# Smaller first loads, tile by tile first products and another order of the head in a mixer and MLP kernel

## The chip, the core and the metric

The kernel runs on one core of a Trainium2 chip. The metric is the device time of one execution in microseconds (us), as a median of several runs. One more execution is taken by the hardware profiler; it gives the profile, and its own time and span are given beside the median. The core has a matmul engine (PE, with its weight loads shown apart as PEld), a vector engine (DVE), an activation engine (ACT), GpSimd (POOL), and SP, which here does nothing but issue DMA transfers.

## The reference

All inputs are bf16: x is 1 x 2048 x 512, w1 and w2 are 512 x 512, w3 is 512 x 1792 and w4 1792 x 512.

```python
h  = gelu(layernorm(x) @ w1)
c  = D // 4                      # four groups of 128 channels
g0 = h[:, :, 0:c]     shifted by +1 row      # zeros come in
g1 = h[:, :, c:2*c]   shifted by -1 row
g2 = h[:, :, 2*c:3*c] shifted by +2 rows
g3 = h[:, :, 3*c:]    shifted by -2 rows
x1 = x + concat(g0, g1, g2, g3) @ w2
out = x1 + gelu(layernorm(x1) @ w3) @ w4
```

The layernorm has no weights; its epsilon is 1e-5, and GELU is the tanh form.

## The kernel before, in words

**Tiling.** The 2048 rows are 16 tiles of 128, taken with a stride: partition p holds rows 16p to 16p+15, tile t is row 16p+t of each partition. A shift by rows is thus mostly a shift to a neighbouring tile. Two tiles make a pair, and the first product (w1) is done by pairs.

**Stages for a tile q of the first layernorm.** A load of x from SP (`load_x`, L253); statistics on DVE (`st`, L325) and their aggregate (`ag`, L328); the reciprocal root on POOL (`rs`, for two tiles at a time or one: an add, L349, and a power, L358); the normalisation on DVE (`norm`, L378) into `xn`. Then a transpose, in one of two ways. Tiles 0 to 7: four transposes on PE into a bank of PSUM (`tp`, L400) and an evacuation on ACT into `xT` (`evA`, L412). Tiles 8 to 15: a DMA transpose that SP issues (`dT`, L388). The first product of a pair (`m1`, L451) is four groups of four matmuls with a moving operand of 256 columns, one group for each 128 output channels. GELU on ACT (`g1`) writes `hT`, which holds the shifts. The second product of a tile (`m2 tile bank channels`, L526) reads `hT` of the pairs that its shifts reach, and `add` on DVE (L538) makes x1.

**After the head** follow x1's statistics, normalisation (mostly on ACT, L373) and DMA transposes, then the wide part: mm3 (L553), GELU (L566), mm4 (L579), the last add (L593) and the store (L597). mm3 starts with w3 and the first four transposed tiles of x1.

**What sets the order.** Each engine runs its instructions in the order in which the program calls the helpers. The helper records each operation with what it reads and writes (`Prog`), and `emit` turns these into semaphore waits. For the head, the order is written out by hand in the string `HEAD` (L160): each step is a name and its numbers, and each engine takes its own steps from it in order. A step stands on one engine only; an engine whose next step waits runs nothing else meanwhile. `dT` steps set SP's order, behind the loads, which stand ahead of the head (L617 to L627).

**Pair 0 before.** Its product is `m1i` (`mm1_by_input`, L459): one step per input chunk of w1, each with four matmuls of 256 columns, into the four banks 0 to 3, so that it can start with the first chunks of w1. It reads both tiles of the pair. `warm` (L604) is 12 and then 3 matmuls of constants ahead of the first transposes.

**Loads before.** x tiles 0, 1, 2 and 3 alone (128 KB each), 4 and 5 together (256 KB), w1 chunks 0 and 1 and then 2 and 3 (256 KB each), x tiles 6 and 7 (256 KB), 8 to 11 and 12 to 15 (512 KB each), w2 (512 KB): eleven transfers.

Of the kernel before, what the change touches and what calls it, by code (L numbers as in the profile page):

```python
# [5 lines left out]
P = 128  # L6
# [151 lines left out]


HEAD = """  # L160
st 0; ag 0; rs 0 1; st 1; ag 1; rs 1 1; st 2; st 3; ag 2; ag 3; warm 3 3 1; rs 2; norm 1; norm 0;
tp 1 5; tp 0 4; st 4; evA 1; norm 2; norm 3; evA 0; tp 2 6; tp 3 7; st 5; ag 4; ag 5; m1i 0 0 0;
evA 3; rs 4; m1i 0 0 1; evA 2; m1i 0 0 2; st 6; m1i 0 0 3; norm 4; m1 1 4 3; norm 5; g1 0;
tp 4 6; st 7; m1 1 4 0; ag 6; ag 7; tp 5 7; rs 6; evA 4; m1 1 4 1; st 9; evA 5; m1 1 4 2; st 8;
norm 7; m1 2 0 1; ag 8; ag 9; g1 1; m1 2 0 3; rs 8; norm 6; tp 7 7; st 11; m1 2 0 2; evA 7;
tp 6 6; norm 8; m1 2 0 0; ag 11; evA 6; m2 2 4 0; m2 2 4 1; st 10; m1 3 2 2; norm 9; ag 10; g1 2;
m1 3 2 0; rs 10; st 13; m1 3 2 1; m1 3 2 3; st 12; m2 2 4 2; dT 8; m2 2 4 3; norm 11; ag 13;
norm 10; g1 3; m2 3 5 0 1 2 3; st 14; ag 12; dT 9; rs 12; st 15; m2 4 6 0 1 2 3; ag 14; ag 15;
m1 4 0 3; rs 14; dT 11; m1 4 0 1; norm 13; m1 4 0 0; add 3; norm 14; dT 10; m2 5 7 0 1 2 3;
add 2; m1 4 0 2; norm 12; norm 15; dT 13; g1 4; dT 12; dT 14; dT 15  # L170
"""


def bass_standalone__mixer_s_mlp__prompt_kernel(
# [13 lines left out]
    DC = D // P  # L188
# [12 lines left out]
    with ExitStack() as es:  # L201
# [3 lines left out]
        xT = sb("xT", [P, DC, S], BF16)  # L205
# [3 lines left out]
        w1_sb = sb("w1_sb", [P, DC, D], BF16)  # L209
# [33 lines left out]
        g_mv = [Gen() for _ in range(2 * NT)]  # L243
# [5 lines left out]
        def bankap(b, n=1):  # L249
            return ps[:, 512 * b : 512 * (b + n)]  # L250


        def load_x(eng, t0, n):  # L253
            pr.op(eng, f"x{t0}",
                  lambda e: e.dma_start(x_sb[:, t0 : t0 + n, :], x3[:, t0 : t0 + n, :]),
                  w=g_x[t0 : t0 + n], dma=True)

        def load_w(name, dst, src, c0=0, n=DC):

            v = src.rearrange("(c p) f -> p c f", p=P)  # L260
            pr.op("sp", f"{name}_{c0}",
                  lambda e: e.dma_start(dst[:, c0 : c0 + n, :], v[:, c0 : c0 + n, :]),
                  w=[g_w[(name, c)] for c in range(c0, c0 + n)], dma=True)
# [103 lines left out]
        def norm(eng, q):  # L367
            a, g = src(q)
            s = q % NXN
            g_xn[q] = xn_slot[s].new()  # L370
            if eng == "act":
                pr.op("act", f"norm{q}",
                      lambda e: e.activation(xn[:, s, :], a, ACT_F.Identity,  # L373
                                             bias=nmr[:, q : q + 1], scale=rstd[:, q : q + 1]),
                      r=[g, g_nmr[q], g_rstd[q]], w=[g_xn[q]])
            else:
                pr.op(eng, f"norm{q}",
                      lambda e: e.tensor_scalar(xn[:, s, :], a, mv[:, q, 0:1], rstd[:, q : q + 1],  # L378
                                                ALU.subtract, ALU.mult),
                      r=[g, g_mv[q], g_rstd[q]], w=[g_xn[q]])  # L380

        def xT_of(q):
            return (xT, q) if q < NT else (x1T, q - NT)
# [22 lines left out]
        def evacT(eng, q):  # L406
            g, b = g_tp[q]
            dst, c = xT_of(q)
            a = ps_bf[:, 1024 * b : 1024 * b + 512].rearrange("p (c s) -> p c s", c=DC)
            o = dst[:, :, P * c : P * (c + 1)]  # L410
            if eng == "act":
                pr.op("act", f"ev{q}", lambda e: e.activation(o, a, ACT_F.Copy), r=[g], w=[g_xT[q]])  # L412
            else:
                pr.op("dve", f"ev{q}", lambda e: e.tensor_copy(o, a), r=[g], w=[g_xT[q]])
# [24 lines left out]
        g_y = {}  # L439
# [16 lines left out]
            pr.op("pe", f"mm1_{p}_{len(fcs)}", f, r=all_of("w1") + [g_xT[2 * p], g_xT[2 * p + 1]],  # L456
                  w=[gens[h] for h in range(2) if any(fc // 2 == h for fc in fcs)])

        def mm1_by_input(p, b, dcs):  # L459

            if p not in g_y:
                g_y[p] = ([bank[b + i].new() for i in range(DC)], b)
            for dc in dcs:
                def f(e, dc=dc):
                    for fc in range(DC):
                        dst = ps[:, 512 * (b + fc) : 512 * (b + fc) + 256]
                        ins = e.matmul(dst, w1_sb[:, dc, P * fc : P * (fc + 1)],
                                       xT[:, dc, 256 * p : 256 * (p + 1)],
                                       start=(dc == 0), stop=(dc == DC - 1))
                    return ins  # L470

                pr.op("pe", f"mm1_{p}_1_{dc}", f,
                      r=[g_w[("w1", dc)], g_xT[2 * p], g_xT[2 * p + 1]], w=g_y[p][0])

        def hap(j, p, jn=1):

# [127 lines left out]
        def keep_warm(n, b, after=()):  # L604

            g = bank[b].new()
            ones = nc.const_aps.tensor(1.0, (P, 512), BF16)

            def f(e):
                for _ in range(n):  # L610
                    ins = e.matmul(bankap(b), ones[:, 0:P], ones, start=True, stop=True)  # L611
                return ins

            pr.op("pe", f"warm{len(after)}", f, r=list(after), w=[g])
# [3 lines left out]
        load_x("sp", 1, 1)  # L618
        load_x("sp", 2, 1)
        load_x("sp", 3, 1)  # L620
        load_x("sp", 4, 2)
        load_w("w1", w1_sb, w1, 0, 2)
        load_w("w1", w1_sb, w1, 2, 2)
        load_x("sp", 6, 2)
        load_x("sp", 8, 4)
        load_x("sp", 12, 4)
        load_w("w2", w2_sb, w2)  # L627
# [58 lines left out]
        def last_tile():  # L686
# [6 lines left out]

        steps = {
            "st": stats, "ag": aggr, "rs": rstd_pool, "norm": lambda q: norm("dve", q), "tp": peT,
            "evA": lambda q: evacT("act", q), "dT": dmaT,
            "m1i": lambda p, b, *dcs: mm1_by_input(p, b, dcs),
            "warm": lambda n, b, q: keep_warm(n, b, [g_mv[q]]),
            "m1": lambda p, b, *fcs: mm1(p, b, fcs), "g1": gelu1,
            "m2": lambda t, b, *js: mm2(t, b, js), "add": add1,  # L700
        }
# [22 lines left out]
        for k in (10, 12, 14):  # L724
            q = NT + k
# [49 lines left out]
```

## Time and profile before

| what | us |
|---|---|
| median of 3 runs (138.76 to 138.92) | 138.88 |
| the profiled execution, its own time | 139.09 |
| its span in the profile | 137.3 |
| PE busy | 131.9 |
| DVE busy | 51.6 |
| ACT busy | 50.0 |
| first transpose on PE / first product on PE / first mm3 on PE | 6.76 / 8.73 / 38.03 |
| PE idle before the first two groups of transposes | 0.48 and 0.70 |
| landing of x tiles 8 to 11, issued at 4.56 | 11.6 |

The span goes from the first instruction to the last. All times in the profile count from its start. A row of a timeline has a start, a length from the first start to the last end, the engine, line and operation with what it writes and reads, the number of instructions, and in brackets the idle time of the engine before it with what ended it. Instructions of one engine overlap in their last part, so the step from one start to the next is shorter than an instruction's own length. "SPq" is the queue on which SP issues transfers; a landing is the time from issue to the last semaphore update. The granted PE clock was 1.0 over the whole profiled execution.

### The profile page before, as it was taken

Reading aid. Unit: us, or ns where it says so; the run is one execution under the profiler, and the core shown is the slowest. Engines: PE = TensorE matmul, PEld = TensorE weight load, DVE = VectorE, ACT = ScalarE, POOL = GpSimd, SP = SyncE. Lnnn points to the kernel's source line nnn. Section 1 sums busy time; section 2 is a strip of 40 time slices with the busy share of each in tenths; the row PEclk is TensorE's granted clock in tenths of the full one; section 3 lists DMA queues with packets and bytes.
Section 4 is the critical chain, followed back from the end, with each engine's and each line's share of the span. In section 5 each row is a group of like instructions: output and inputs, shape, how many; then the busy total and the mean of one; then the engine's idle time right before and its main releaser. Section 6 shows DMA issues by size and latency. Waiting matters only on the chain.

```text
span 137.3 us, 1790 instructions
## 1 busy us (share of the span) xinstructions
PE 131.9 (96%) x689; PEld 66.5 (48%) x701; DVE 51.6 (38%) x125; ACT 50.0 (36%) x60; POOL 18.3 (13%) x52
## 2 busy tenths in 40 slices
PE   7879999999999999999999999999999999999993
PEld 3267847664444444444444444444444444444452
DVE  0989899999976620000232000023200002232222
ACT  4068622399545555552000555300055530000000
POOL 2542442464312200000000000000000000000000
PEclk9999999999999999999999999999999999999999
DMA  4996144589955599300111100011110001111121
GB/s 106 289 283 238 27 93 82 111 261 351 133 100 113 83 287 257 103 5 0 38 38 38 38 0 5 0 38 38 38 38 0 5 0 38 38 38 38 38 74 41
DMA packets 20119, 12.16 MB, mean 89 GB/s; under 512 B 13712, under 2 KB 19088, under 8 KB 20112
## 3 DMA queue, kind: packets, MB, share of 16 engines
q1 hardware_dynamic: 19968, 12.03, 33.6%
q8 instruction: 5, 0.08, 0.3%
q10 hardware_dynamic: 144, 0.03, 0.1%
q14 instruction: 2, 0.02, 0.0%
HBM read 6.82 MB, written 2.10 MB: 65 GB/s over the span
## 4 chain that ended last, share of the span: by engine, by line
PE 83%; DVE 8%; DMA 4%; POOL 1%; issue 1%; DVEq 0%
PE ps L579 35%; PE ps L553 35%; PE ps L526 8%; PE ps L451 5%; DVE st L325 5%; DVE xn L378 2%; DMA x_sb<-in_x_dram 2%; DMA xT<-xn 2%; POOL rstd L358 1%; DVE mv L328 1%; POOL vpe L349 0%; DVE o_sb L593 0%; DVEq L134 0%
## 5 line engine op out<-in xcount | busy, mean ns | idle before, releaser
L579 PE MATMUL ps<-w_sb,h2T 128*128 128x512 bf16 (+2 forms) x234 | 48.7, 366 | 0.2
L553 PE MATMUL ps<-x1T,w_sb 128*128 128x512 bf16 x219 | 48.6, 379 | 0.3
L566 ACT ACTIVATE h2T<-ps 128x1024 bf16<-128x1024 f32 x28 | 28.6, 1023 | 44.8 <-PE ps L553 44.8
L593 DVE TENSOR_TENSOR o_sb<-ps,x_sb 128x512 bf16<-128x512 f32 (+2 forms) x17 | 11.2, 660 | 75.0 <-PE ps L579 75.0
L579 PEld LDWEIGHTS ps<-w_sb,h2T 128*128 128x128 bf16 x238 | 22.8, 98 | 25.9
L553 PEld LDWEIGHTS ps<-x1T,w_sb 128*128 128x128 bf16 x224 | 21.9, 98 | 26.4
L325 DVE BATCH_NORM_STATS2 st<-x_sb 128x6 f32<-128x512 bf16 x32 | 20.7, 675 | 2.3 <-DMA x_sb<-in_x_dram 2.3
L526 PE MATMUL ps<-w_sb,hT 128*128 128x512 bf16 x61 | 14.3, 379 | 0.2
L451 PE MATMUL ps<-xT,w_sb 128*128 128x256 bf16 x112 | 14.0, 273 | 0.3 <-DMA xT<-xn 0.3
L451 PEld LDWEIGHTS ps<-xT,w_sb 128*128 128x128 bf16 x112 | 10.6, 98 | 3.1 <-issue 0.7
L358 POOL TENSOR_TENSOR rstd<-vpe,neghalf 128x2 f32<-128x2 f32 (+1 forms) x17 | 11.8, 695 | 1.0
L538 DVE TENSOR_TENSOR x_sb<-ps,x_sb 128x512 bf16<-128x512 f32 x16 | 10.3, 678 | 0.3 <-PE ps L526 0.2
L378 DVE TENSOR_SCALAR xn<-x_sb,mv,rstd 128x512 bf16<-128x512 bf16 x22 | 8.3, 405 | 5.2 <-POOL rstd L358 5.0
L526 PEld LDWEIGHTS ps<-w_sb,hT 128*128 128x128 bf16 x64 | 6.2, 98 | 6.3 <-ACT hT L512 0.3
L373 ACT ACTIVATE xn<-x_sb,nmr,rstd 128x512 bf16<-128x512 bf16 x10 | 7.6, 807 | 3.3 <-POOL nmr L363 3.3
L512 ACT ACTIVATE hT<-ps 128x1024 bf16<-128x1024 f32 x6 | 6.1, 1019 | 6.1 <-PE ps L451 6.0
L349 POOL TENSOR_SCALAR vpe<-mv 128x2 f32<-128x2 f32 (+1 forms) x17 | 3.9, 229 | 27.3 <-DVE mv L328 27.2
L412 ACT ACTIVATE xT<-ps 128x512 bf16<-128x512 bf16 x8 | 4.5, 603 | 5.9 <-PE ps L400 5.9
L611 PE MATMUL ps<-const-bfloat16-1.0 128*128 128x512 bf16 x15 | 5.4, 522 | 0.9 <-PEq L760 0.8
L328 DVE BATCH_NORM_AGGREGATE mv<-st 128x2 f32<-128x6 f32 x32 | 4.9, 172 | 0.1
L400 PE MATMUL ps<-ident,xn 128*128 128x128 bf16 x32 | 3.0, 221 | 1.2 <-DVE xn L378 1.2
L611 PEld LDWEIGHTS ps<-const-bfloat16-1.0 128*128 128x128 bf16 x15 | 1.8, 127 | 4.0 <-issue 3.2
(18 smaller groups left out, 12.8 us busy)
## 6 DMA issues: line engine op xcount, KB each, us to landing
w_sb<-in_w_dram SPq DMA_DIRECT2D x4, 512.0 KB, 4.8
out_dram<-o_sb SPq DMA_DIRECT2D x15, 128.0 KB, 1.8
w_sb<-in_w_dram SPq DMA_DIRECT2D x1, 1792.0 KB, 7.3
x_sb<-in_x_dram SPq DMA_DIRECT2D x2, 512.0 KB, 7.5
w_sb<-in_w_dram SPq DMA_DIRECT2D x3, 256.0 KB, 4.1
x_sb<-in_x_dram SPq DMA_DIRECT2D x4, 128.0 KB, 2.5
x_sb<-in_x_dram SPq DMA_DIRECT2D x2, 256.0 KB, 4.1
x1T<-xn SPq DMA_TRANSPOSE x16, 3.6
```

Of the source, the lines that this page charges most:

```text
L325: pr.op("dve", f"st{q}", lambda e: e.bn_stats(st6[:, q, :], a), r=[g], w=[g_st[q]])
L358: lambda e: e.tensor_tensor(rstd[:, q : q + n], vpe[:, q : q + n], neghalf[:, 0:n], ALU.pow),
L373: lambda e: e.activation(xn[:, s, :], a, ACT_F.Identity, bias=nmr[:, q : q + 1], scale=rstd[:, q : q + 1]),
L378: lambda e: e.tensor_scalar(xn[:, s, :], a, mv[:, q, 0:1], rstd[:, q : q + 1], ALU.subtract, ALU.mult),
L451: ins = e.matmul(dst, w1_sb[:, dc, P * fc : P * (fc + 1)], xT[:, dc, 256 * p : 256 * (p + 1)], start=(dc == 0), stop=(dc == DC - 1))
L526: ins = e.matmul(bankap(b), hT[:, j, c : c + P], w2_sb[:, j, :], start=(j == 0), stop=(j == DC - 1))
L538: lambda e: e.tensor_tensor(x1_sb[:, t, :], bankap(b), x_sb[:, t, :], ALU.add),
L553: ins = e.matmul(bankap(b + i), w3_sb[:, dc, P * fc : P * (fc + 1)], x1T[:, dc, 512 * s : 512 * (s + 1)], start=(dc == 0), stop=(dc == DC ...
L566: pr.op("act", f"g2_{s}_{fp}", lambda e: e.activation(o, a, ACT_F.Gelu_apprx_tanh), r=gens, w=[g])
L579: ins = e.matmul(ps[:, 512 * b : 512 * b + n], h2T[:, fc, s % 2, P * i : P * (i + 1)], w4_sb[:, fc, c0 : c0 + n], start=(fc == 0), stop=(f ...
L593: lambda e: e.tensor_tensor(o_sb[:, s, 0:n], ps[:, 512 * b : 512 * b + n], x1_sb[:, t, c0 : c0 + n], ALU.add),
L611: ins = e.matmul(bankap(b), ones[:, 0:P], ones, start=True, stop=True)
```

## The change

It has three parts. The loads of x tiles 0 to 7 and of w1's four input chunks become twelve transfers of 128 KB, in the order x0, x1, x2, x3, x4, w1 chunk 0, chunk 1, x5, chunk 2, chunk 3, x6, x7; the three transfers of 512 KB behind them stay. `mm1_by_input` gives way to `mm1_tile_by_input`: the first products of tiles 0 and 1 are made for each tile by itself, four steps of four matmuls with 128 columns, into halves of the same banks 0 to 3. And `HEAD` is written anew: tile 0's normalisation, transpose and evacuation come ahead of tile 1's, tile 0's product stands ahead of transposes 3 and 2, and tile 1's product is mixed with them; tile 4's transpose is evacuated by DVE (`evD`) in place of ACT; the order of statistics, normalisations, groups of `m1` and `m2` and of the DMA transposes (9 ahead of 8) differs down to the end of the head, where `add 3` and `add 2` now stand behind all of the normalisations. What follows the head is as it was.

```diff
 HEAD = """
-st 0; ag 0; rs 0 1; st 1; ag 1; rs 1 1; st 2; st 3; ag 2; ag 3; warm 3 3 1; rs 2; norm 1; norm 0;
-tp 1 5; tp 0 4; st 4; evA 1; norm 2; norm 3; evA 0; tp 2 6; tp 3 7; st 5; ag 4; ag 5; m1i 0 0 0;
-evA 3; rs 4; m1i 0 0 1; evA 2; m1i 0 0 2; st 6; m1i 0 0 3; norm 4; m1 1 4 3; norm 5; g1 0;
-tp 4 6; st 7; m1 1 4 0; ag 6; ag 7; tp 5 7; rs 6; evA 4; m1 1 4 1; st 9; evA 5; m1 1 4 2; st 8;
-norm 7; m1 2 0 1; ag 8; ag 9; g1 1; m1 2 0 3; rs 8; norm 6; tp 7 7; st 11; m1 2 0 2; evA 7;
-tp 6 6; norm 8; m1 2 0 0; ag 11; evA 6; m2 2 4 0; m2 2 4 1; st 10; m1 3 2 2; norm 9; ag 10; g1 2;
-m1 3 2 0; rs 10; st 13; m1 3 2 1; m1 3 2 3; st 12; m2 2 4 2; dT 8; m2 2 4 3; norm 11; ag 13;
-norm 10; g1 3; m2 3 5 0 1 2 3; st 14; ag 12; dT 9; rs 12; st 15; m2 4 6 0 1 2 3; ag 14; ag 15;
-m1 4 0 3; rs 14; dT 11; m1 4 0 1; norm 13; m1 4 0 0; add 3; norm 14; dT 10; m2 5 7 0 1 2 3;
-add 2; m1 4 0 2; norm 12; norm 15; dT 13; g1 4; dT 12; dT 14; dT 15
+st 0; st 1; ag 0; rs 0 1; st 2; ag 1; st 3; rs 1 1; norm 0; ag 2; ag 3; warm 3 3 1; tp 0 4; rs 2;
+st 4; norm 1; evA 0; tp 1 5; st 5; m1x 0 0 0; ag 4; ag 5; m1x 0 0 1; evA 1; rs 4; norm 3;
+m1x 0 0 2; m1x 0 0 3; norm 2; tp 3 7; m1x 1 0 0; tp 2 6; st 6; evA 3; m1x 1 0 1; norm 5;
+m1x 1 0 2; norm 4; m1x 1 0 3; evA 2; tp 5 7; tp 4 6; st 7; ag 7; evA 5; m1 1 4 0; evD 4; ag 6;
+m1 1 4 2; g1 0; rs 6; m1 1 4 3; st 8; m1 1 4 1; st 9; ag 8; m1 2 0 2; ag 9; rs 8; norm 6;
+m1 2 0 1; g1 1; norm 7; m1 2 0 3; tp 6 6; st 10; tp 7 7; norm 9; evA 6; m1 2 0 0; m2 2 4 0;
+st 11; m2 2 4 1; evA 7; ag 10; ag 11; m2 2 4 2; rs 10; norm 8; m1 3 2 0; g1 2; st 13; m1 3 2 3;
+m1 3 2 2; st 12; m1 3 2 1; norm 11; dT 9; m2 2 4 3; st 15; ag 12; ag 13; g1 3; m2 3 5 0 1 2 3;
+rs 12; norm 10; dT 8; st 14; ag 14; ag 15; m2 4 6 0 1 2 3; rs 14; norm 13; m1 4 0 3; dT 11;
+m1 4 0 0; m1 4 0 2; norm 14; norm 12; norm 15; dT 10; m2 5 7 0 1 2 3; m1 4 0 1; add 3; add 2;
+dT 13; g1 4; dT 12; dT 14; dT 15
 """
...
+        def mm1_tile_by_input(t, b, dc):
+
+            p = t // 2
             if p not in g_y:
                 g_y[p] = ([bank[b + i].new() for i in range(DC)], b)
+            def f(e):
+                for fc in range(DC):
+                    o = 512 * (b + fc) + P * (t % 2)
+                    ins = e.matmul(ps[:, o : o + P], w1_sb[:, dc, P * fc : P * (fc + 1)],
+                                   xT[:, dc, P * t : P * (t + 1)],
+                                   start=(dc == 0), stop=(dc == DC - 1))
+                return ins
+
+            pr.op("pe", f"m1x_{t}_{dc}", f, r=[g_w[("w1", dc)], g_xT[t]], w=g_y[p][0])
...
-        load_x("sp", 4, 2)
-        load_w("w1", w1_sb, w1, 0, 2)
-        load_w("w1", w1_sb, w1, 2, 2)
-        load_x("sp", 6, 2)
+        load_x("sp", 4, 1)
+        load_w("w1", w1_sb, w1, 0, 1)
+        load_w("w1", w1_sb, w1, 1, 1)
+        load_x("sp", 5, 1)
+        load_w("w1", w1_sb, w1, 2, 1)
+        load_w("w1", w1_sb, w1, 3, 1)
+        load_x("sp", 6, 1)
+        load_x("sp", 7, 1)
         load_x("sp", 8, 4)
         load_x("sp", 12, 4)
         load_w("w2", w2_sb, w2)
...
-            "evA": lambda q: evacT("act", q), "dT": dmaT,
-            "m1i": lambda p, b, *dcs: mm1_by_input(p, b, dcs),
-            "warm": lambda n, b, q: keep_warm(n, b, [g_mv[q]]),
+            "evA": lambda q: evacT("act", q), "evD": lambda q: evacT("dve", q), "dT": dmaT,
+            "warm": lambda n, b, q: keep_warm(n, b, [g_mv[q]]), "m1x": mm1_tile_by_input,
```

More of the change, by code (lines that the diff above doesn't have):

```diff
@@ L457, in mm1 @@
                   w=[gens[h] for h in range(2) if any(fc // 2 == h for fc in fcs)])
-        def mm1_by_input(p, b, dcs):
+        def mm1_tile_by_input(t, b, dc):
+            p = t // 2
             if p not in g_y:
                 g_y[p] = ([bank[b + i].new() for i in range(DC)], b)
[L463 to L473, printed above, removed]
+            def f(e):
[6 more added lines that the diff above has]
+            pr.op("pe", f"m1x_{t}_{dc}", f, r=[g_w[("w1", dc)], g_xT[t]], w=g_y[p][0])
         def hap(j, p, jn=1):
```

## The prediction

> **What bounds the kernel now.** I read the page first, then the chain of waits, then the timelines of PE and DVE over the first 26 us, then the landings of the loads. The page's busy line, slices and chain:
>
> ```profile
> PE 131.9 (96%) x689; PEld 66.5 (48%) x701; DVE 51.6 (38%) x125; ACT 50.0 (36%) x60; POOL 18.3 (13%) x52
> PE   7879999999999999999999999999999999999993
> DVE  0989899999976620000232000023200002232222
> PE 83%; DVE 8%; DMA 4%; POOL 1%; issue 1%; DVEq 0%
> ```
>
> PE is busy in every slice from the fourth on (one slice is 3.4 us). A change in the head can therefore bring only what it takes out of PE's first 10 us and of any later hole. The chain still runs through DVE for 8%: the head is DVE preparing tiles (statistics, normalise) for PE. The waits, as total us, times, longest:
>
> ```profile
> DVE xn L378 <- POOL rstd L358: 5.0, 6, 1.2
> DVE st L325 <- DMA x_sb<-in_x_dram: 2.3, 1, 2.3
> PE ps L400 <- DVE xn L378: 1.2, 2, 0.7
> PE ps L451 <- DMA xT<-xn: 0.3, 1, 0.3
> ```
>
> After its warm-up matmuls PE has three holes: two before transposes (0.48 and 0.70 us), one of 0.25 us for a DMA transpose. On PE's timeline and DVE's (start, length, work, idle before):
>
> ```profile
> 6.76 0.72 PE L400 MATMUL ps<-ident,xn 128*128 128x128 bf16 x8 [0.48 <-DVE xn L378]
> 8.18 0.72 PE L400 MATMUL ps<-ident,xn 128*128 128x128 bf16 x8 [0.70 <-DVE xn L378]
> 8.73 1.91 PE L467 MATMUL ps<-xT,w_sb 128*128 128x256 bf16 x16
> 10.48 0.60 PE L451 MATMUL ps<-xT,w_sb 128*128 128x256 bf16 x4
> 10.95 0.40 PE L400 MATMUL ps<-ident,xn 128*128 128x128 bf16 x4
> ...
> 19.82 1.47 PE L451 MATMUL ps<-xT,w_sb 128*128 128x256 bf16 x12 [0.25 <-DMA xT<-xn]
> ```
>
> ```profile
> 4.93 1.25 DVE L325 BATCH_NORM_STATS2 st<-x_sb 128x6 f32<-128x512 bf16 x2
> 6.10 0.30 DVE L328 BATCH_NORM_AGGREGATE mv<-st 128x2 f32<-128x6 f32 x2
> 6.32 0.70 DVE L378 TENSOR_SCALAR xn<-x_sb,mv,rstd 128x512 bf16<-128x512 bf16 x2
> ...
> 7.71 0.73 DVE L378 TENSOR_SCALAR xn<-x_sb,mv,rstd 128x512 bf16<-128x512 bf16 x2
> ```
>
> The first product starts at 8.73, behind all four transposes, and from there to the first mm3 at 38.03 PE stops once, for 0.25 us. From 38.03 to 134.95 there are no holes but some of 0.05 us. So the end moves with the time at which mm3 starts.
>
> **The change, part by part.**
>
> *PE's work.* Tiles 0 and 1 are multiplied one at a time, 32 matmuls of 128 columns in place of 16 of 256. The 16 start at 8.73 and the next work at 10.48, 0.109 us each. For 128 columns the nearest row is the transpose, which also loads new weights each time: four take 0.40 us, of which the last one's own length is 0.22 (mean 221 ns), so 0.06 apart, 0.056 on the finer reading (8 in 0.72 with a pause between). 32 x 0.056 = 1.79 us against 1.75: +0.04 us. Bounds: no less than half of 0.109 each, since as many columns pass in all (0), and no more than 0.109 each (+1.74); the transpose row is the nearest in shape and loads weights as often, so I take 0.04.
>
> *The order at the start.* DVE before did tiles 0 to 3's statistics, then norm 1 and norm 0 at 6.32, and norm 2 and 3 at 7.71. Steps between starts, from DVE's timeline: statistics 0.585 (two from 4.93 to 6.10), aggregate 0.10 to 0.12, norm 0.32 (two from 7.71 to 8.36), a step that waits for the one just ahead of it 0.73 instead of 0.60. After: st 0 at 3.31, st 1 3.90 (x1 has landed at 3.7), ag 0 4.48, st 2 4.58, ag 1 5.17, st 3 5.27, norm 0 5.86. Its rstd is ready: aggregate end to pow end was 4.22 to 5.20 and is now 4.66 to 5.64. Norm 0 ends at 6.27 (0.41 long), transpose 0 starts at 6.33; its evacuation on ACT (0.43 after the transpose starts, 0.60 long) ends at 7.37. Then ag 2, ag 3, st 4 (6.4), norm 1 at 7.0 to 7.4, transpose 1 at 7.46. It is queued ahead of the first product, which starts at 7.68 (four times 0.056 later). So the **first product starts 1.05 us earlier**, 7.68 for 8.73.
>
> Transposes 2 and 3 (0.45 us) now stand behind it. Walked on: tile 0's product to 8.58; norm 3 and 2 at 8.1 and 8.45, so transpose 3 at 8.58 and, behind tile 1's first part, transpose 2 at 9.02 come without a hole; tile 1's product ends at 9.92; norm 5 waits for POOL until 9.5 (aggregate end 8.2 plus 1.3), transposes 5 and 4 run to 10.5 with about 0.1 us of holes; pair 1's 16 matmuls to 12.25; three quarters of pair 2 to 13.55. Norms 6 and 7 start at 12.9 and 13.2 and transposes 6 and 7 end at 14.0. Pair 2's rest, three mm2 and pair 3 fill PE to 16.85, mm2 of tiles 2 and 3 to 17.92. Tile 4's mm2 needs pair 3's GELU (PE 16.85 + 0.2, ACT 1.02 long): 18.1, a hole of 0.2. It ends at 18.97. Next is pair 4, which before started at 19.82.
>
> So the sum: +1.05 (first product), +0.25 (the hole at 19.82), -0.45 (two transposes that now come after), -0.04, and -0.1 to -0.3 of new small holes: **0.5 to 0.8 us; I take 0.7**, as the walk to 18.97 gives 0.85 and the bounds below cut it.
>
> *What must keep up.* Pair 4 needs DMA transposes of tiles 8 and 9. They are now issued tile 9 first, at norm 9's end (14.6), the second 1.3 to 1.7 us later (the issues at 15.52 and 17.21 were 1.69 apart, later ones 1.31), landing 2.5 to 2.8 after issue: 18.4 to 19.1, against PE's 18.97. Before, the second landed at 19.69. Later transposes are issued back to back and follow in step. At mm3 the fourth transpose of x1 landed at 37.48, 0.55 ahead of PE. It hangs on DVE: adds 3 and 2 (0.60 each) now run after norm 15, and I get st 16 at 23.8 against 24.16. So that landing comes 0.4 earlier, and at most some 0.8 us of gain passes there.
>
> *DVE and ACT.* Tile 4's evacuation goes from ACT (0.49 us a step) to DVE: one more step of 0.32 (norm's row) to 0.60 (the add's, which also reads PSUM); I take 0.60. It stands ahead of ag 6 and st 8, so DVE reaches st 8 at 11.6; the cover is that PE has pair 1 to work on until 12.25. Without cover it would cost 0.6. DVE before sat idle for POOL three times (0.64, 0.37, 0.34 us); the new order keeps one, about 0.9 us at norm 14, behind which only late tiles stand.
>
> *Twelve transfers on SP's queue.* Before, eleven loads; now fifteen. An issue takes 0.47 us (five from 0.73 to 3.06), so x tiles 8 to 11, 12 to 15 and w2 are issued 1.8 us later: 6.35, 6.8 and 7.3 for 4.56, 5.04 and 5.51. The page's landings (KB each, median us from issue):
>
> ```profile
> x_sb<-in_x_dram SPq DMA_DIRECT2D x2, 512.0 KB, 7.5
> w_sb<-in_w_dram SPq DMA_DIRECT2D x3, 256.0 KB, 4.1
> x_sb<-in_x_dram SPq DMA_DIRECT2D x4, 128.0 KB, 2.5
> x_sb<-in_x_dram SPq DMA_DIRECT2D x2, 256.0 KB, 4.1
> ```
>
> Small transfers land 2.5 us after issue, each at SP's pace; larger ones queue (taken one by one: tiles 4 and 5 at 6.2, w1 at 6.9 and 7.6, tiles 6 and 7 at 8.5, tiles 8 to 11 at 11.6, 12 to 15 at 12.9, w2 at 14.2). By 2.5 us, now: tile 4 at 5.1, w1's chunks 5.6, 6.0, 7.0, 7.4, tile 5 6.5, tiles 6 and 7 at 7.9 and 8.4. All are ahead of use (tile 5 at 7.3, chunk 3 at 8.3, tile 6 at 8.8). Tiles 8 to 11 then take 1.4 us (512 KB at the 360 to 389 GB/s of 9.5 to 11 us) to 3.1 (what they took, 8.5 to 11.6): 9.8 to 11.5, needed at 11.6. w2 lands 2.6 later, 12.4 to 14.1, needed at 14.3. So late issue is hidden by the backlog that the queue had anyway, with 0.1 to 1.8 us to spare. If the cover is gone, each us past it costs one us.
>
> A rule speaks against this. In the Trainium skill, "DMA: Bandwidth & Descriptors", section "Rules for kernel authors", small transfers are to be coalesced and 1 MiB is asked for full bandwidth. The trace agrees in part: the four 128 KB landings are 0.44 us apart, near 300 GB/s, the 256 KB ones some 0.77, near 340. By the rule alone the loads would end later and the second rival below would decide.
>
> **The rivals.**
>
> *The gain stops at a transpose.* PE already waits for a DMA transpose at 19.82. One of them took 3.5 us instead of 2.5 and one of x1's took 5.2, so a landing 0.6 to 1.0 us late at tile 8, tile 10 or x1's fourth leaves 0 to 0.25 us of gain: 138.85 to 139.1 in the profiled execution's terms. For it: that wait exists. Against: the issues move 0.8 us earlier with the norms. Chance 0.15.
>
> *Loads come late: slower.* If tiles 8 to 11 keep their 7.1 us from issue, they land at 13.45 instead of 11.62. St 8 then starts 1.85 us later than in the walk, and norms 6 to 9 stand behind it on DVE. PE runs out at 13.55 and all that follows moves: 1.85 less 0.1 of spare, less the 0.7 of gain, so 1.05 us slower, 140.1 in the profiled execution's terms. It decides from a landing at 12.4 on (or from tile 5 or a w1 chunk 1.5 us late). For it: four more issues ahead, 1 KB pieces in place of 2 KB. Against: the 7.1 us were mostly queue, and the queue is fed earlier with the same bytes. Chance 0.25.
>
> *It does nothing that matters at the start* (the first product waits for w1 or for transpose 1 until 8.5): about 0.2 us, inside the first rival's outcome and counted there.
>
> **How the numbers follow.** The profiled execution took 139.09 us, 137.3 of it span, 1.8 around it. 139.09 - 0.7 = 138.4. The median shown is 138.88, 0.21 lower, so 138.2 for a median. The forecast has 0.60 (its own range 137.8 to 138.6, gains of 0.3 to 1.1), the first rival 0.15 (near 138.8), the second 0.25 (138.9 to 139.9 by the median). About 0.2%, 0.28 us, can be told from no change. Faster 0.60, same 0.15, slower 0.25. The range runs from 137.8 to 139.6; the slow rival's far end is left out.
>
> **What would show it.** Right: first product on PE near 7.7, no PE hole over 0.3 us after it, mm3 near 37.3, tiles 8 to 11 landing before 11.6. Wrong: a wait of DVE's statistics for a load after 10 us; a PE hole near 13.5 or 14.3; a wait for a transpose at 19 or at mm3; matmuls of 128 columns more than 0.06 apart.

## The result, and the profile after

The median after is 139.66 us (139.02 to 140.32, 22 runs) against 138.89 before (138.44 to 140.0, 22 runs), a ratio of 1.0048 with a 95% interval of [1.0031, 1.0066]: slower by about half a per cent, where 0.7 us of gain was forecast. Three executions of one kernel below, e8, ran at a granted clock of 0.988 in place of 1.0 and are left out. The profiled execution took 140.0 us, of which 137.4 are span. Around the span are therefore 2.6 us; before it was 139.09 less 137.3, 1.8. Two things are to be explained: why the span did not shrink, and why the time around it grew.

The page of the changed kernel: busy time, two engines' slices, the chain.

```profile
PE 132.7 (97%) x705; PEld 67.1 (49%) x717; DVE 51.9 (38%) x126; ACT 49.5 (36%) x59; POOL 18.7 (14%) x52
PE   7989899999999999999999999999999999999993
DVE  1997998999976620000232000023200002232222
PE 80%; DVE 8%; DMA 4%; SPq 4%; issue 1%; POOL 1%; DVEq 0%
```

PE's fifth slice, about 13.7 to 17.2 us, is now an 8, so there is a hole there that before did not have. SPq is new in the chain: SP's issues themselves stand on it. PE's timeline (start, length, work, idle before):

```profile
0.76 6.24 PE L612 MATMUL ps<-const-bfloat16-1.0 128*128 128x512 bf16 x15 [0.76 <-PEq L764]
6.84 0.84 PE L401 MATMUL ps<-ident,xn 128*128 128x128 bf16 x8
8.00 1.05 PE L469 MATMUL ps<-xT,w_sb 128*128 128x128 bf16 x16 [0.32 <-ACT xT L413]
...
14.53 0.60 PE L452 MATMUL ps<-xT,w_sb 128*128 128x256 bf16 x4
15.68 0.59 PE L527 MATMUL ps<-w_sb,hT 128*128 128x512 bf16 x2 [0.55 <-PE ps L452]
...
38.22 2.10 PE L554 MATMUL ps<-x1T,w_sb 128*128 128x512 bf16 x9
```

The first product did move, from 8.73 to 8.00. Yet mm3 starts at 38.22, against 38.03. From first product to mm3 are now 30.2 us, and there is a hole of 0.55 ahead of the first mm2, the first reader of w2. DVE's timeline and then the chain that ended last show one late load, x tiles 8 to 11:

```profile
12.11 1.29 DVE L326 BATCH_NORM_STATS2 st<-x_sb 128x6 f32<-128x512 bf16 x2 [0.63 <-DMA x_sb<-in_x_dram]
```

```profile
5.91 0.43 SPq L256
6.38 5.71 DMA x_sb<-in_x_dram
12.11 1.29 DVE st L326 x2
```

The landings by the page (KB each, median us from issue), and below them w2's own, issued at 7.33, from the DMA view of 7.2 to 7.6 us:

```profile
x_sb<-in_x_dram SPq DMA_DIRECT2D x8, 128.0 KB, 2.8
x_sb<-in_x_dram SPq DMA_DIRECT2D x2, 512.0 KB, 6.4
w_sb<-in_w_dram SPq DMA_DIRECT2D x4, 128.0 KB, 3.0
```

```profile
w_sb<-in_w_dram SPq DMA_DIRECT2D x1, 512.0 KB, 8.0
```

Tiles 8 to 11 were issued at 6.38 and landed at 12.09, where the forecast had 9.8 to 11.5. DVE stood idle 0.63 us for them. w2 landed at 15.37, where 12.4 to 14.1 was forecast. The row of the hole names PE's own earlier work as its releaser; but that work (four matmuls from 14.53) ended at 15.13, and the hole goes on to 15.68. Experiment e15 below shows that it is w2. The transposes of tiles 8 to 15, the adds and mm3 follow PE without a new wait.

Outside the span, the DMA view from 138 to 140 us of the changed kernel holds a single packet, on a queue that carries instructions (8 KB; the second line has 40 slices of 0.05 us, so it lies near 139.7, 2.3 us behind the span's end):

```profile
DMA packets 1, 0.01 MB, mean 4 GB/s; under 512 B 0, under 2 KB 0, under 8 KB 0
GB/s 0 0 0 0 0 0 0 0 0 0 0 0 0 0 0 0 0 0 0 0 0 0 0 0 0 0 0 0 0 0 0 0 0 0 164 0 0 0 0 0
q14 instruction: 1, 0.01, 1.5%
```

In before the same view, from 136.5 to 141 us, is empty:

```profile
DMA packets 0, 0.00 MB, mean 0 GB/s; under 512 B 0, under 2 KB 0, under 8 KB 0
```

### The profile page after: what moved, and what is told of

It is laid out like the page before. It is cut to its first block, busy times and chain, and to the rows that moved or that the text cites. A ratio compares the mean times of both kernels' runs of the same rounds, so it can differ in the third digit from the quotient of the medians.

```text
span 137.4 us, 1829 instructions
## 1 busy us (share of the span) xinstructions
PE 132.7 (97%) x705; PEld 67.1 (49%) x717; DVE 51.9 (38%) x126; ACT 49.5 (36%) x59; POOL 18.7 (14%) x52
## 4 chain that ended last, share of the span: by engine, by line
PE 80%; DVE 8%; DMA 4%; SPq 4%; issue 1%; POOL 1%; DVEq 0%
PE ps L580 35%; PE ps L554 35%; PE ps L527 7%; DMA x_sb<-in_x_dram 4%; DVE st L326 3%; PE ps L452 3%; SPq L256 2%; DVE xn L379 2%; DVE x_sb L539 2%; SPq L263 1%; DVE mv L329 1%; POOL rstd L359 1%; DVE o_sb L594 0%; POOL vpe L350 0%; DVEq L134 0%
## 5 line engine op out<-in xcount | busy, mean ns | idle before, releaser
L527 PE MATMUL ps<-w_sb,hT 128*128 128x512 bf16 x61 | 14.5, 379 | 0.7 <-PE ps L452 0.6
L452 PE MATMUL ps<-xT,w_sb 128*128 128x256 bf16 x112 | 13.4, 273 | 0.0
L612 PE MATMUL ps<-const-bfloat16-1.0 128*128 128x512 bf16 x15 | 6.1, 578 | 0.9 <-PEq L764 0.8
L413 ACT ACTIVATE xT<-ps 128x512 bf16<-128x512 bf16 x7 | 3.9, 595 | 6.9 <-PE ps L401 6.9
```

The lines of the kernel that those rows point to most:

```text
L452: ins = e.matmul(dst, w1_sb[:, dc, P * fc : P * (fc + 1)], xT[:, dc, 256 * p : 256 * (p + 1)], start=(dc == 0), stop=(dc == DC - 1))
L527: ins = e.matmul(bankap(b), hT[:, j, c : c + P], w2_sb[:, j, :], start=(j == 0), stop=(j == DC - 1))
```

## The experiments

**The theories.** The first: the loads come late, since SP issues four more of them ahead of tiles 8 to 11 and of w2. Its rival: the 32 matmuls of 128 columns, or the new order of the head, cost more on PE than forecast. The first four kernels tell these apart. They showed that neither accounts for the time around the span, so a third was formed: the longer program on SP's queue costs time behind the last store.

For each kernel the table gives the median, the ratio to the kernel before on the same chip, the mean span of its runs beside that of the runs of before on the same chip, and the mean of time less span ("around"). Beside the changed kernel itself no spans of before were taken. "SP" is the number of SP's records in the trace.

| kernel | us | ratio | span, before's | around | SP |
|---|---|---|---|---|---|
| before, four chips | 138.58 to 138.71 | 1 | 136.74 to 137.02 | 1.82 to 1.83 | 69 |
| after | 139.66 | 1.0048 [1.0031, 1.0066] | 137.25 | 2.41 | 73 |
| e1 | 138.70 | 0.9993 [0.998, 1.0005] | 136.87, 136.89 | 1.81 | 69 |
| e2 | 139.59 | 1.0056 [1.0038, 1.0073] | 137.23, 136.89 | 2.35 | 73 |
| e3 | 138.80 | 1.0005 [0.9993, 1.0017] | 136.99, 136.89 | 1.82 | 69 |
| e4 | 138.68 | 0.9994 [0.998, 1.0008] | 136.61, 136.89 | 2.07 | 74 |
| e5 | 139.04 | 1.003 [1.0012, 1.0048] | 136.72, 136.80 | 2.35 | 73 |
| e6 | 139.02 | 1.0028 [1.001, 1.0047] | 137.21, 136.80 | 1.81 | 69 |
| e7 | 138.11 | 0.9956 [0.9938, 0.9973] | 136.23, 136.80 | 1.82 | 69 |
| e8 (3 runs) | 139.51 | 1.007 | 137.57, 136.80 | 1.84 | 69 |
| e9 | 138.79 | 1.0019 [1.0005, 1.0033] | 137.00, 136.74 | 1.81 | 71 |
| e10 | 138.52 | 1.000 [0.9988, 1.0012] | 136.74, 136.74 | 1.82 | 70 |
| e11 | 139.72 | 1.0087 [1.0068, 1.0107] | 137.32, 136.74 | 2.35 | 73 |
| e12 | 139.59 | 1.0076 [1.0053, 1.0099] | 137.08, 136.74 | 2.51 | 73 |
| e13 | 139.07 | 1.0023 [0.9999, 1.0047] | 137.38, 137.02 | 1.82 | 81 |
| e14 | 138.75 | 0.9996 [0.9977, 1.0014] | 136.96, 137.02 | 1.80 | 71 |
| e15 | 138.98 | 1.0011 [0.9993, 1.0029] | 137.13, 137.02 | 1.85 | 69 |
| e16 | 138.65 | 0.9985 [0.9964, 1.0006] | 136.75, 137.02 | 1.83 | 69 |

### One part of the change at a time: e1 to e4

**e1**: before, with pair 0's first product as 32 matmuls of 128 columns and nothing else changed.

```diff
-                        dst = ps[:, 512 * (b + fc) : 512 * (b + fc) + 256]
-                        ins = e.matmul(dst, w1_sb[:, dc, P * fc : P * (fc + 1)],
-                                       xT[:, dc, 256 * p : 256 * (p + 1)],
...
+                t = 2 * p + dc // 2
+                cs = (0, 1) if dc % 2 == 0 else (2, 3)
...
+                            o = 512 * (b + fc) + P * (t % 2)
+                            ins = e.matmul(ps[:, o : o + P], w1_sb[:, c, P * fc : P * (fc + 1)],
+                                           xT[:, c, P * t : P * (t + 1)],
```

> The kernel before with pair 0's first product as 32 matmuls of 128 columns, tile 0 and then tile 1, at the places where its 16 stood; loads and order untouched. Theory 1 (the loads are late: tiles 8 to 11 landed at 12.1 and w2 at 15.4 in the profile after, and DVE and PE waited for them): no change, 138.9, mm3 at 38.0 to 38.1. Theory 2 (the loss lies outside the span: in the profiled executions the time around the span was 2.6 us after and 1.8 before, and PE has 32 instructions more, 16 matmuls and 16 weight loads): slower by 0.5 to 0.8, 139.4 to 139.7, with the same span of 137.3 and some 2.6 around it.

The time did not move, and the 32 matmuls took 1.95 us from first start to last end (0.055 to 0.056 a step), against 1.91 for the 16. So the matmuls cost the 0.04 us that the prediction took, and the rival falls in its first half.

**e2**: before, with the twelve small loads only.

```diff
-        load_x("sp", 4, 2)
-        load_w("w1", w1_sb, w1, 0, 2)
-        load_w("w1", w1_sb, w1, 2, 2)
-        load_x("sp", 6, 2)
+        load_x("sp", 4, 1)
+        load_w("w1", w1_sb, w1, 0, 1)
+        load_w("w1", w1_sb, w1, 1, 1)
+        load_x("sp", 5, 1)
+        load_w("w1", w1_sb, w1, 2, 1)
+        load_w("w1", w1_sb, w1, 3, 1)
+        load_x("sp", 6, 1)
+        load_x("sp", 7, 1)
```

> The kernel before with the twelve 128 KB transfers of the change and nothing else of it. Theory 1: tiles 8 to 11 land near 12.1, 0.4 later than DVE needs them in the old order, and w2 near 15.4, 0.4 later than PE needs it: slower by 0.2 to 0.5, 139.1 to 139.4, mm3 at 38.2 to 38.5. Theory 2: PE has no instruction more, so no change or the 0.2 that the landings cost: 138.9 to 139.1 with 1.8 around the span.

The loads by themselves give the whole loss: 0.34 us in the span and 0.53 around it. DVE's and PE's timelines name both late transfers:

```profile
11.96 1.29 DVE L325 BATCH_NORM_STATS2 st<-x_sb 128x6 f32<-128x512 bf16 x2 [0.23 <-DMA x_sb<-in_x_dram]
```

```profile
15.37 0.61 PE L526 MATMUL ps<-w_sb,hT 128*128 128x512 bf16 x2 [0.26 <-DMA w_sb<-in_w_dram]
```

**e3**: the changed kernel with before's eleven loads (the diff of e2 the other way round).

> The kernel after with the loads of the kernel before (tiles 4 and 5, w1 by two chunks, tiles 6 and 7 as 256 KB transfers); its order and its 128-column products stay. Theory 1: with tiles 8 to 11 at 11.6 and w2 at 14.2, as in the profile before, the walk gives mm3 at 37.3 to 37.5: faster than before by 0.5, near 138.4. Theory 2: the span falls by 0.5 but 0.7 to 0.8 stay outside it: 138.9 to 139.2.

Without the small loads nothing is lost around the span, and nothing is won in it: DVE now waits for tiles 4 and 5 and for tiles 6 and 7, which come as pairs:

```profile
6.55 0.69 DVE L326 BATCH_NORM_STATS2 st<-x_sb 128x6 f32<-128x512 bf16 x1 [0.40 <-DMA x_sb<-in_x_dram]
...
9.31 0.69 DVE L326 BATCH_NORM_STATS2 st<-x_sb 128x6 f32<-128x512 bf16 x1 [0.31 <-DMA x_sb<-in_x_dram]
```

So the new order waits where the small loads would have been there in time, and the small loads make the next ones late. In this profile the warm-up also ended late: the first transpose starts at 6.91 and the first product at 8.07, and what part that has in e3's missing gain isn't shown. The order by itself costs nothing that the runs can tell (ratio 1.0005), which is the other half of the rival.

**e4**: the changed kernel with tiles 8 and 9 alone first behind the twelve, and w2 ahead of tiles 12 to 15.

```diff
-        load_x("sp", 8, 4)
-        load_x("sp", 12, 4)
+        load_x("sp", 8, 2)
+        load_x("sp", 10, 2)
         load_w("w2", w2_sb, w2)
+        load_x("sp", 12, 4)
```

> The kernel after with what stands behind the twelve transfers in another order and size: tiles 8 and 9 (256 KB), 10 and 11 (256 KB), w2, then 12 to 15. Theory 1: tiles 8 and 9 land near 10.6, ahead of DVE at 11.4, and w2 near 14, ahead of PE at 14.9, so both waits go and mm3 starts near 37.3: faster than before by 0.5 to 0.7, 138.2 to 138.4. Theory 2: the same gain in the span, lost outside it: 138.9 to 139.2.

Tiles 8 and 9 landed at 10.91, w2 at 13.48. Both waits are gone on DVE and PE:

```profile
11.39 1.25 DVE L326 BATCH_NORM_STATS2 st<-x_sb 128x6 f32<-128x512 bf16 x2
```

```profile
8.00 1.05 PE L469 MATMUL ps<-xT,w_sb 128*128 128x128 bf16 x16 [0.31 <-ACT xT L413]
...
14.71 0.81 PE L527 MATMUL ps<-w_sb,hT 128*128 128x512 bf16 x3
...
37.51 1.67 PE L554 MATMUL ps<-x1T,w_sb 128*128 128x512 bf16 x7
```

With the same first product at 8.00, mm3 starts at 37.51 instead of 38.22. The two late landings therefore cost 0.71 us between these two profiles, and over the runs the span is 0.28 below before's. Yet the time is before's, because 0.25 more lie around the span: the third theory's question.

### The time around the span: e5, e6, e9, e10, e13, e14

**e5**: before, with w4 in eight transfers in place of four, late, when nobody is short of them.

```diff
-            load_w4(2 * (k - 10), 4)
+            load_w4(2 * (k - 10), 2), load_w4(2 * (k - 10) + 2, 2)
...
-        load_w4(12, FC - 12)
+        load_w4(12, 1), load_w4(13, 1)
```

> The kernel before with w4 loaded in eight transfers in place of four, far behind the head and 5 us ahead of use; head, order and first loads untouched. SP so issues four transfers more, as many as in the kernel after. Theory 2b (four more instructions on SP's queue lengthen what lies around the span: the three kernels with 15 or 16 early loads had 2.1 to 2.5 us there, and an 8 KB packet of the instruction queue after the span, those with 11 had 1.8 and none): span unchanged at 136.9, around it 2.1 to 2.5, time 139.0 to 139.4. Theory 1b (what lies around the span has to do with the early loads themselves): span 136.9, around it 1.8, time 138.7.

The span stayed (136.72 for 136.80), the time around it went from 1.82 to 2.35, and the packet is there, at 138.84. Four more transfers late on SP's queue do it as well as four early ones; the head has no part in it.

**e6**: the changed kernel with four of its last stores issued by ACT, so that SP is back at 69 records.

```diff
-                    add2(k)
+                    add2(k, queue="act" if k > 10 else "sp")
```

> The kernel after with four of the last stores (of tiles 11 to 14 in the order of the end) issued by ACT, which has nothing else to do by then; SP has again as many instructions as in the kernel before, the program as many transfers and semaphores as after. Theory 2b: the span stays at 137.2, around it falls to 1.8, time 139.0 to 139.1. If it is the number of transfers or semaphores in the program that counts, and not SP's queue: around it stays at 2.4, time 139.6.

The time around the span is 1.81 again and the packet is gone, with as many transfers in the program as in the changed kernel: it is SP's queue that counts. (e8, whose w1 is issued by ACT, has 69 records on SP too, 1.84 around the span and no packet.) What remains, 0.41 us of span above before's, is the loss inside.

**e9 and e10**: before, with four and with two waits more on SP, on semaphores that have long been reached (they became two records and one). **e13**: with 24.

```diff
+            for o in [o for o in order if o.dma and o.name.startswith("out")][:4]:    # e10: [:2]
+                nc.sync.wait_ge(sems[o.stream], 16)
```

```diff
+            for o in 2 * [o for o in order if o.dma and o.name.startswith("out")][:12]:
+                nc.sync.wait_ge(sems[o.stream], 16)
```

> The kernel before with four more semaphore waits on SP, put ahead of its 17 closing waits and on stores that have long landed, so that they wait for nothing; no transfer and no semaphore more. If the number of SP's instructions makes the time around the span: span 136.8, around it 2.3 to 2.4 and an 8 KB packet of the instruction queue behind the span, time 139.1 to 139.2. If it is the number of transfers that SP issues: around it 1.8, time 138.6 to 138.7.

> As the one with four more waits, with two. If SP's instructions count and the border lies in the upper half between 69 and 73 records: 1.8 around the span, 138.6 to 138.7; in the lower half: 2.3 to 2.4, 139.1 to 139.2. An effect that grows with each instruction would give 2.1.

> The kernel before with 24 more semaphore waits on SP, two to an instruction, so twelve instructions (81 records on SP for 69), ahead of the closing waits and on stores that have landed; no transfer more. If the number of SP's instructions makes the time around the span: 2.0 to 2.5 around it, an 8 KB packet behind the span, time 139.1 to 139.3. If it takes transfers: 1.8, time 138.6 to 138.8.

**e14**: before, with two of w4's loads halved, two transfers more.

```diff
-            load_w4(2 * (k - 10), 4)
+            load_w4(2 * (k - 10), 4) if k == 10 else (load_w4(2 * (k - 10), 2), load_w4(2 * (k - 10) + 2, 2))
```

> The kernel before with two of w4's loads halved: two transfers more (71 records on SP), where four more gave 2.4 around the span and 73 records. A border between 71 and 73 records: 1.8 around it, 138.6. An effect of each transfer: 2.1, 138.9. A border below 71 for transfers, unlike waits: 2.4, 139.1.

At 70 and 71 records (e10, e9, e14) there is no packet and 1.80 to 1.82 us lie around the span; at 73 and 74 (after, e2, e4, e5, e11, e12) there are a packet and 2.07 to 2.51. The border is thus between 71 and 73 of SP's records, and more transfers than before are on both sides of it. At 74 records (e4) the packet comes 1.9 us behind the span in place of 2.3, and the time around is the least of the six, 2.07. e13 went past it with waits alone, and the packet came, but at 137.3, 0.3 us behind the span's end in place of 2.3 (DMA view of e13, 136.5 to 141 us, slices of 0.11 us):

```profile
GB/s 0 0 0 0 0 0 0 73 0 0 0 0 0 0 0 0 0 0 0 0 0 0 0 0 0 0 0 0 0 0 0 0 0 0 0 0 0 0 0 0
```

There the time around the span stayed at 1.82, but the span is 0.36 us longer, and the trace shows where. These are two of SP's closing records behind its last wait for a store (duration in ns, start in us), in e13 and then in e9:

```profile
L110 SPq COMPARE_BRANCH  x1: 33/33/33, 136.3 to 136.3; - x1
L110 SPq DRAIN  x1: 85/85/85, 136.7 to 136.7; - x1
```

```profile
L110 SPq COMPARE_BRANCH  x1: 33/33/33, 136.2 to 136.2; - x1
L110 SPq DRAIN  x1: 7/7/7, 136.4 to 136.4; - x1
```

The branch stands at nearly the same place, so the 24 waits held nothing up; the drain comes some 0.3 us later behind it, and the end of the span with it. So it looks as if the cost did not go away but moved from behind the span into its last steps. That fits a fetch of SP's instructions that costs time wherever SP reaches it with no work left to cover it. It does not prove it: e13's packet is recorded at 137.3, behind those steps. The 0.26 us of e9's span, whose end looks like before's, stay open. What is shown is the link between four transfers more on SP, the packet behind the span and 0.5 to 0.6 us, in e5 and e6 from both sides.

In the Trainium skill, "Runtime: NRT & Kernel Launch", section "Instruction fetch mechanics", an engine's instructions are fetched in blocks by a DMA queue of its own, and the cost of crossing a block is called mostly hidden. The first half is what the packet looks like; if the packet is the cause, the second doesn't hold at the end of this program, where the time around the span grew by 0.5 to 0.6 us of 139.

### What is left inside the span: e8, e11, e12, e15, e16

**e8**: the changed kernel with w1's four chunks issued by ACT, to free SP.

```diff
-        def load_w(name, dst, src, c0=0, n=DC):
+        def load_w(name, dst, src, c0=0, n=DC, eng="sp"):
...
-            pr.op("sp", f"{name}_{c0}",
+            pr.op(eng, f"{name}_{c0}",
...
-        load_w("w1", w1_sb, w1, 0, 1)
+        load_w("w1", w1_sb, w1, 0, 1, "act")
...
```

> The kernel after with w1's four chunks issued by ACT, ahead of its table load, so that SP issues eleven loads as before and x tiles 8 to 11 go out near 4.5 instead of 6.4. If SP's pace of issue makes them late: tiles 8 to 11 land near 10.2 to 11, w2 near 13.5, DVE and PE wait for neither, span 136.4 to 136.7. If the transfers themselves take this long (1 KB pieces, the engines busy): landings as after, 12.1 and 15.4, and the span stays at 137.2. Around it 1.8 by theory 2b, 2.4 if the number of transfers counts: 138.2 to 138.5 in the best case, 139.6 in the worst.

Chunks 1 to 3 go to ACT likewise. SP issued tiles 8 to 11 at 4.48, they landed at 10.21 and w2 at 13.75, ahead of their use. The transfers are as small as in the changed kernel, so this points to SP's pace of issue as what makes the later loads late, and not to the size of the pieces. But the first tile landed at 3.69 instead of 2.96, the third at 5.13 instead of 4.21, and the first product started at 8.32. With two queues issuing at once, the transfers that are needed first came later and the others sooner. The three runs took 138.95, 139.51 and 139.75 us, with spans of 137.1 to 137.9: no gain.

**e11**: the changed kernel with w2 ahead of tiles 12 to 15, nothing else. **e15**: with tiles 8 and 9 first, but w2 last (and five stores on ACT, as in e7).

```diff
         load_x("sp", 8, 4)
-        load_x("sp", 12, 4)
         load_w("w2", w2_sb, w2)
+        load_x("sp", 12, 4)
```

```diff
-        load_x("sp", 8, 4)
+        load_x("sp", 8, 2)
+        load_x("sp", 10, 2)
...
-                    add2(k)
+                    add2(k, queue="act" if k > 9 else "sp")
```

> The kernel after with w2 issued ahead of x tiles 12 to 15, nothing else. If w2's landing costs the span (PE waited for it at 15 in the profile after): w2 lands near 14, tiles 12 to 15 near 15.4, which DVE needs at 15.6 to 16; the span falls by 0.2 to 0.4, to 136.9 to 137.0, time 139.3. If tiles 8 to 11 alone cost it (DVE waits for them at 12): span as after, 137.2, time 139.6. In both, 2.4 around it.

> The kernel after with x tiles 8 and 9 and tiles 10 and 11 as two transfers, w2 still last, and the last five of SP's stores on ACT, which keeps SP at 69 records. If the landing of tiles 8 to 11 alone costs the span: span 136.6 to 136.7 as with w2 ahead, 1.8 around it, 138.4 to 138.5. If w2 costs it too: 136.9 to 137.1, 138.7 to 138.9.

Each of the two late transfers is enough by itself to undo e4's gain: e4's span is 0.28 below before's, e15's (w2 late) 0.11 above it and e11's (tiles 8 to 11 late) 0.58 above. In e11 w2 was early (13.41), tiles 8 to 11 were not (11.97), and the span stayed where the changed kernel's is. On PE, e15 has e4's rows from 8.00 to 14.3 us, with w2 at 15.45 instead of 13.48:

```profile
14.27 0.60 PE L452 MATMUL ps<-xT,w_sb 128*128 128x256 bf16 x4
15.76 0.59 PE L527 MATMUL ps<-w_sb,hT 128*128 128x512 bf16 x2 [0.89 <-PE ps L452]
...
38.30 1.89 PE L554 MATMUL ps<-x1T,w_sb 128*128 128x512 bf16 x8
```

The first mm2 starts 0.31 us behind w2's landing, as in the changed kernel (15.37 and 15.68), and 1.05 later than in e4. That is how one learns that the releaser named in brackets, PE's own work, wasn't it. (The profiled execution was e15's longest of 12, 137.5 of span for a mean of 137.13, so its 38.30 is a late sample.)

Which of the two holds PE up last differs between executions. In the changed kernel's profile it is w2. e6 has the same head and the same loads; there the warm-up ended sooner, the first product started at 7.22, w2 landed at 14.54, and PE stood still for the other load: DVE waits for tiles 8 to 11, and normalisations 6 and 7, which transposes 6 and 7 need, stand behind the statistics of tiles 8 and 9. First e6's DVE, then its PE:

```profile
11.96 1.29 DVE L326 BATCH_NORM_STATS2 st<-x_sb 128x6 f32<-128x512 bf16 x2 [0.95 <-DMA x_sb<-in_x_dram]
```

```profile
7.22 1.06 PE L469 MATMUL ps<-xT,w_sb 128*128 128x128 bf16 x16
...
13.81 0.72 PE L401 MATMUL ps<-ident,xn 128*128 128x128 bf16 x8 [0.51 <-DVE xn L379]
```

In e6 mm3 starts at 37.62. A first product 0.78 us earlier than e4's thus brought mm3 no sooner than e4's 37.51. From first product to mm3 it takes 30.2 to 30.7 us in the four kernels with tiles 8 to 11 in one transfer behind the twelve (after, e6, e11, e12), and 29.5 in e4.

**e12**: the changed kernel without the second step of warm-up matmuls. **e16**: e7 (below) with that step put back.

```diff
-st 0; st 1; ag 0; rs 0 1; st 2; ag 1; st 3; rs 1 1; norm 0; ag 2; ag 3; warm 3 3 1; tp 0 4; rs 2;
+st 0; st 1; ag 0; rs 0 1; st 2; ag 1; st 3; rs 1 1; norm 0; ag 2; ag 3; tp 0 4; rs 2;
```

> The kernel after without the second warm-up step of three matmuls. If that step, in PE's queue ahead of transpose 0, holds up the first product, and the loads then take the gain: first product at 7.2 to 7.6 in place of 8.0, but the end is set by tiles 8 to 11 and w2, so the span falls by 0 to 0.2 (137.0 to 137.2), time 139.4 to 139.6. If the end hangs on the first product all the same: span 136.7 to 136.9, 139.1 to 139.3.

> The best version so far (faster than before by 0.44%, span 136.2 for 136.8) with the second warm-up step back ahead of transpose 0. If that step costs what it holds up: span 136.5 to 136.7, 138.3 to 138.5. If the gain came from loads and stores alone: 136.2, 138.1.

In e12 the first product started at 7.24, and the time stayed that of the changed kernel (139.59): tiles 8 to 11 landed at 12.29, and PE stood 0.55 us ahead of transposes 6 and 7, as in e6. The 0.76 us against the changed kernel's 8.00 are not the price of the step alone, since e6 and e11, which have it, started at 7.22 and 7.29. With loads on time the edit counts: e7's span is 0.57 below before's, e16's 0.27, so the step costs some 0.3 us. From 6 and 12 runs on two chips that is known to no better than 0.25 us.

### A kernel that beats both: e7

**e7**: the changed kernel with e4's loads, without that warm-up step, and with SP's last five stores on ACT.

```diff
-... norm 0; ag 2; ag 3; warm 3 3 1; tp 0 4; rs 2;
+... norm 0; ag 2; ag 3; tp 0 4; rs 2;
...
-        load_x("sp", 8, 4)
-        load_x("sp", 12, 4)
+        load_x("sp", 8, 2)
+        load_x("sp", 10, 2)
         load_w("w2", w2_sb, w2)
+        load_x("sp", 12, 4)
...
-                    add2(k)
+                    add2(k, queue="act" if k > 9 else "sp")
```

> The kernel after with tiles 8 and 9, 10 and 11, w2 and then 12 to 15 behind the twelve transfers, with the last five stores that SP issued issued by ACT, and without the second warm-up step of three matmuls, behind which transpose 0 stood in PE's queue till 6.84 though norm 0 had ended at 6.2. Theory 2b with 1: the span falls to 136.1 to 136.4 (136.6 less up to 0.5 for the earlier first product) and 1.8 around it: 137.9 to 138.3, faster than before by 0.4 to 0.8. If the warm-up is needed for the clock, transposes and first products run at half rate and the span grows by 0.5 to 1. If SP's queue is not the cause, 2.1 around it: 138.2 to 138.6.

138.11 us, 0.9956 [0.9938, 0.9973] of before. Most of the gain that was forecast for the change's order is there (0.57 us of span) once the loads, the warm-up and SP's queue let it through:

```profile
7.22 1.06 PE L469 MATMUL ps<-xT,w_sb 128*128 128x128 bf16 x16
...
14.56 0.59 PE L527 MATMUL ps<-w_sb,hT 128*128 128x512 bf16 x2
...
37.16 3.19 PE L554 MATMUL ps<-x1T,w_sb 128*128 128x512 bf16 x14
```

No wait stands ahead of the first mm2, and mm3 starts 1.06 us earlier than in the changed kernel. DVE still waits 0.49 us for tiles 8 and 9 (landed 11.47), so there is some more to be had.

## Why the prediction was wrong

It forecast 138.2 us and faster; it came to 139.66 and slower. Step by step:

- **"So late issue is hidden by the backlog that the queue had anyway"** is the step that failed within the span. The prediction's loads would end no later than before, at 9.8 to 11.5 for tiles 8 to 11 and 12.4 to 14.1 for w2; they landed at 12.09 and 15.37, 0.5 and 1.1 us later than in before's profile. Other profiles say the same: with before's loads tiles 8 to 11 land at 10.8 to 11.8 us and w2 at 13.4 to 14.4, with the new ones at 11.9 to 12.3 and, where w2 stands behind all of x, at 14.5 to 15.5. The small transfers were slower than the 2.5 us taken from before's row, 2.8 and 3.0 by the page (tile 7 at 8.96, not 8.4), and tiles 8 to 11 came 3.1 us behind them, the far end of what the prediction had allowed (3.4 in e6). It had counted on engines kept full by the queue. The busy times by stretches of 1 us show that they weren't (last two columns: the engines' mean busy share and GB/s), in before first and then in the changed kernel:

```profile
8.00:9.00 1.00, 0.82 (x11) 0.71 (x12) 1.00 (x4) 0.34 (x2) 0.00 (x0) 1.00 0.97 260
9.00:10.00 1.00, 1.00 (x12) 0.90 (x10) 0.84 (x4) 1.00 (x2) 0.57 (x2) 1.00 0.87 320
10.00:11.00 1.00, 1.00 (x11) 0.78 (x10) 0.52 (x2) 0.34 (x2) 0.37 (x1) 1.00 0.99 385
```

```profile
8.00:9.00 1.00, 1.00 (x18) 1.00 (x19) 1.00 (x4) 0.34 (x1) 0.74 (x2) 1.00 0.70 226
9.00:10.00 1.00, 1.00 (x21) 1.00 (x19) 0.92 (x3) 0.69 (x2) 0.28 (x1) 1.00 0.68 205
10.00:11.00 1.00, 1.00 (x19) 0.91 (x16) 0.94 (x4) 0.75 (x2) 0.00 (x0) 1.00 0.84 313
```

In the changed kernel the engines stand at 0.7 from 8 to 10 us, where the small transfers run out and the large ones, issued from 6.38 on, only begin. In before the large ones, issued 1.8 us earlier, were the backlog: their first 4 KB packet runs at 6.9 us, in the changed kernel at 7.5. The price is 0.71 us at mm3 (e4 against after), which is all the gain forecast. The slow rival had this mechanism, with 13.45 for tiles 8 to 11 as its landing and w2 left out. Its range, 138.9 to 139.9, holds the 139.66, but by luck: most of the loss that was measured is the next item, which it didn't have.
- **"137.3 of it span, 1.8 around it"**, and then only the span was summed. The time around it was taken as fixed and grew by 0.59 us (1.82 to 2.41), through SP's four records more (e5, e6). No step and no rival had it, and no view of before's trace shows it; it is most of the measured loss of 0.67 us (means 139.66 and 138.99). Inside the span the loss is then 0.1 us in that comparison, and 0.34 to 0.41 by e2 and e6.
- **"The first product starts 1.05 us earlier, 7.68"**: it started at 8.00 in the changed kernel's profile. The walk forgot that 15 warm-up matmuls stand in PE's queue ahead of transpose 0. Normalisation 0 was there at 6.2, as forecast, and the warm-up ended near 6.8. How long it runs depends on when its pace doubles: the step between warm-up matmuls falls from 0.427 to 0.22 us near 3.4 us in e2's and e6's profiles, near 4.5 in before's, and in after's it is still 0.427 at 5.4 and is 0.22 by 6.2. Profiles with this head and its first twelve loads therefore start anywhere from 7.22 (e6) to 8.00 (after, e4, e15). That 7.68 lies between them is luck.
- **The base.** 8.73 for before's first product was a late sample. Five other profiles with before's head (e5, e9, e10, e13, e14) have 8.32 to 8.44 and start mm3 at 37.34 to 37.58, not 38.03. Measured from there, some 0.35 of the 1.05 us were never to be had. The prediction corrected its base by 0.21 for the median, but took the gain itself from the one sample.
- **What held.** The 128-column matmuls cost what was said (e1). Tile 4's evacuation on DVE took 0.39 to 0.42 us in place of 0.60; no run tries it alone. The two transposes behind the first product cost about their 0.45: first product to mm3 is 29.5 us in e4 and 29.0 to 29.1 in e9 and e10. The DMA transposes kept up, so the first rival (the gain stops at a transpose) did not come. The rule on small transfers from the Trainium skill, "DMA: Bandwidth & Descriptors", section "Rules for kernel authors", spoke against this change and was right about its direction: the loads did end later, at 15.37 instead of 14.2. e8 points to the pace of issue as the reason.

The sum with measured terms, inside the span: first product 0.38 earlier than before's usual 8.38, less 0.45 to 0.5 for the transposes now behind it, less 0.71 for the late landings, gives a loss of about 0.8 by single profiles; the runs say 0.1 to 0.4. Single profiles of one kernel's head differ by as much at mm3 (before's 38.03 against 37.34 to 37.58, the changed kernel's 38.22 against e6's 37.62), so the runs' figure stands, and how it is shared out between the terms is known to no better than 0.3 us.

## What to carry to other kernels

When loads are cut into smaller ones, walk the landing of the transfers behind them by the issue pace (here 0.47 us each), not by the backlog that the larger ones had, and put the transfer that is needed next first among those behind. Count the records on a queue that issues transfers too, and look at time less span in the runs: a cost there is in no view of the span. And take the instant from which a gain is measured from several profiles, if there are several kernels that share that part.

## What the runs showed of the hardware

- Between 71 and 73 records on SP the time around the span went from 1.80 to 1.82 us up to 2.35 to 2.51 (2.07 at 74 in e4), with one 8 KB packet of the instruction queue behind the span. Four stores moved to ACT took it away (1.81, e6). At 81 records (e13) the time around was 1.82 and the span 0.36 longer.
- With w1 issued from a second queue the first x tile landed at 3.69 us (e8, one profile), against 2.96 in the changed kernel, 3.29 in before and 2.87 to 2.98 in the other profiles: a second queue did not leave the first one's transfers alone.
- The instant at which TensorE's warm-up matmuls double their pace moved from near 3.4 us (e2, e6) to between 5.4 and 6.2 (after, e4) between executions whose first 3 us on PE are the same; three warm-up matmuls in PE's queue ahead of real work cost some 0.3 us (e7 against e16, to no better than 0.25).
